# A rescheduled opening: a fused attention and feed-forward kernel whose first two batches are put into another order on every engine

## Chip, cores, metric

The kernel runs on one core of a Trainium2 chip. The metric is the device time of one execution in microseconds (us). Profiles (traces) are of one execution each; the span of a profile is shorter than the timed figure of the same execution (414.2 and 416.01 us for the kernel before). Engines: PE is TensorE, DVE is VectorE, ACT is ScalarE, POOL is GpSimd (which issues the loads), SP is SyncE.

## The reference

Attention over 8 batches, 8 heads, 576 positions, head dimension 64, with a bias that depends on the distance of two positions; then a bilinear feed-forward.

```python
scores = q @ k.T / 8 + bias          # per batch and head; bias from a table of 32 buckets
attn   = exp(scores - max); attn /= sum(attn)
x      = (attn @ v) rearranged to [4608 tokens, 512]
out    = ((x @ w_a) * (x @ w_b)) @ w_out          # w_a, w_b: 512 x 1536, w_out: 1536 x 512
```

## The kernel before

It works on 32 head pairs (four to a batch). The exp of the bias is a table W; scores go through exp on ACT and are multiplied by W on DVE. A load "lands" when the profile shows its end and whoever waits for it may start. The feed-forward of a chunk of 512 tokens is woven between the attention of later batches: groups of four matmuls "pa" (x times w_a) and "pb" (x times w_b), a copy "ha" on ACT, a product "g" on DVE, and output groups "po". The first chunk can start when batch 0 is through; until then PE is short of work. So the first 72 us are written down as a list of tokens, which is the order in which every engine gets its instructions:

```python
opening = """
    <k0 <q0 <q123h0 <tk <k23 <k1 <W0 <v0 <vtb <Wtb <W1 <W3 <vta <W2 <tq <R1 <q123h1 <v1 <R0 <Wta
    <wa0 <wb0 TK0 PD0 CK0:A PD1 w1 TQ0 PU1 CQ00:D CQ01:D w4 S000 w2 PU0 TQ20 E000 PC1 TQ10 S001 CQ20:D
    ...
    N00 TZ0 E301 M100 X00 S201 CX00:D AV10 wa4 E201 M200 N10 CZ0:A M201 X10 TQ11 M301 CX10:A T0 CQ11:A
    ...
    S310 CX20:A MT1 X30 E110 AV01 CX30:D M111 FA0a E310 M110 S210 FB0a N01 HA0a S211 E210 FA1a G0a
    AV11 HA1a M210 E211 X01 T2 N11 TZ0x CX01:A T3 ET2 FB1a M211 X11 FA2a G1a CX11:A S311 MT2 HA2a
    ...
"""
```

`<x` issues a load; `TQ`/`TK` are transposes of Q and K on PE, `CQ`/`CK` their copies (`:A` on ACT, `:D` on DVE); `S`, `E`, `M` scores, exp and product with the table; `T`, `ET`, `MT` the same for the 64 tail positions; `AV` probabilities times V, `N` its normalisation, `X` and `CX` the transposes and copies of x; `FA`, `HA`, `FB`, `G` the feed-forward (`a`, `b`: halves of 256 tokens, `f`: all 512); `w4` four dummy matmuls of 512 columns, `wa4` the same written to the bank of "av" (the results of `AV`); `PU`, `PC`, `PV`, `PF`, `PX`, `PD` zero fills. "pb" in this text is the first `FB`: from there on PE has the feed-forward as filling.

```python
    def load_weights(src, dst, part):                       # <wa0, <wb0: 512 KB each
        nc.gpsimd.dma_start(out=dst[part][:, :, :],
            in_=src[:, WC * part:WC * part + WC].rearrange("(m p) n -> p m n", p=128))
    ...
    def ff_o_out(c, tt):                                    # one output block of 128 tokens
        ob = wrk.tile([128, DM], FP32, tag="ob", name=f"ob{c}_{tt}")    # two buffers in turn
        nc.scalar.activation(out=ob[:, :], in_=ff["po", tt][:, :], func=ACTF.Copy)
        if c < B:
            r0 = S * c + 128 * tt
            nc.scalar.dma_start(out=out[r0:r0 + 128, :], in_=ob[:, :])
```

The softmax here doesn't subtract the row's maximum and nothing guards it: scores larger than these inputs give would overflow.

## Time and profile before

| | before |
|---|---|
| timed, median of 3 (range) | 417.34 (416.81 to 418.78) |
| timed, the profiled execution | 416.01 |
| span of the profile | 414.21 |
| matmuls, of these dummies | 3497, 22 |
| shape changes of the array | 177 |
| sum of PE's slots | 397.82 |
| first pb starts | 27.94 |
| first w_b block landed | 27.89 |

A slot is the time from one matmul's start to the next when nothing is waited for; "excess" is what a start comes later than its slot says. 1.2 us before the first matmul, the slots, the excess, and 4.2 us after the last matmul's start make up the span.

### The profile page before, as it was taken

The numbers are of one execution on the slowest core, as the hardware profiler recorded it, in microseconds if no ns is written. First come the engines' busy times: TensorE is split into PE (matmuls) and PEld (weight loads), VectorE is DVE, ScalarE is ACT, GpSimd is POOL, SyncE is SP. The second block draws the span as 40 slices with busy tenths as digits, with TensorE's granted clock in tenths as the row PEclk, the third lists the DMA queues.
The fourth block names the chain that finished last, engine by engine and source line by source line (L and its number), as shares of the span: only waits on it lengthen the run. The fifth ranks groups of instructions, "written<-read, shape, count | busy, mean of one in ns | idle before, by whom it ended". The sixth has DMA issues, their size and how long they took to land.

```text
span 414.2 us, 8826 instructions
## 1 busy us (share of the span) xinstructions
PE 403.8 (97%) x3497; PEld 210.9 (51%) x3497; DVE 241.1 (58%) x568; ACT 251.3 (61%) x388; POOL 133.5 (32%) x191
## 2 busy tenths in 40 slices
PE   8789999999999999999999999999999999999996
PEld 3467664545454455544555555554545555444443
DVE  5778887466764665477646774567646652421320
ACT  4988876486647676676667665866476742322321
POOL 7956546399209500870059003400000000000000
PEclk9999999999999999999999999999999999999999
DMA  9999999999949943996099707940421012002004
GB/s 116 171 210 191 205 157 144 164 142 138 123 96 163 121 82 71 150 128 112 15 162 157 112 16 140 124 92 17 101 82 16 17 40 78 0 2 102 1 2 101
DMA packets 135786, 42.05 MB, mean 102 GB/s; under 512 B 113688, under 2 KB 130968, under 8 KB 135744
## 3 DMA queue, kind: packets, MB, share of 16 engines
q0 software_dynamic: 81712, 20.27, 54.6%
q1 hardware_dynamic: 48592, 11.87, 18.1%
q10 hardware_dynamic: 5440, 9.34, 6.8%
q8 instruction: 27, 0.44, 0.5%
q14 instruction: 15, 0.12, 0.1%
HBM read 39.18 MB, written 9.45 MB: 117 GB/s over the span
## 4 chain that ended last, share of the span: by engine, by line
PE 90%; DMA 3%; POOL 2%; ACT 2%; issue 1%; ACTq 0%; DVE 0%
PE pb L633 23%; PE pa L633 23%; PE po L670 22%; PE av L569 7%; PE qk L406 7%; DMA wb<-in_moe_w_b_dram 3%; PE av L559 2%; PE av L563 2%; PE qkt L479 1%; POOL W L235 1%; DMA bias_tab<-wo 1%; PE trb L306 1%; PE trb L415 1%; PE warm L220 1%; ACT att L514 1%
## 5 line engine op out<-in xcount | busy, mean ns | idle before, releaser
L430 ACT ACTIVATE at<-qk 128x1024 bf16<-128x1024 f32 x112 | 113.5, 1030 | 26.4 <-PE qk L406 10.6
L643 DVE TENSOR_TENSOR g<-pb,ha 128x512 bf16<-128x512 f32 (+1 forms) x116 | 75.9, 654 | 74.7 <-PE pb L633 46.8
L633 PE MATMUL pb<-xn,wb 128*128 128x512 bf16 (+1 forms) x464 | 112.5, 365 | 0.8 <-DMA wb<-in_moe_w_b_dram 0.8
L633 PE MATMUL pa<-xn,wa 128*128 128x512 bf16 (+1 forms) x464 | 112.5, 365 | 0.0
L640 ACT ACTIVATE ha<-pa 128x512 f32<-128x512 f32 (+1 forms) x116 | 66.7, 575 | 65.0 <-PE pa L633 65.0
L670 PE MATMUL po<-wo,g 128*128 128x512 bf16 x420 | 99.0, 379 | 0.0
L435 DVE TENSOR_TENSOR at<-at,W 128x1024 bf16<-128x1024 bf16 x112 | 74.8, 684 | 18.2 <-ACT at L430 18.2
L633 PEld LDWEIGHTS <-wa 128*128 128x128 bf16 x464 | 42.0, 98 | 46.2 <-issue 6.0
L633 PEld LDWEIGHTS <-wb 128*128 128x128 bf16 x464 | 41.4, 97 | 43.0 <-issue 4.7
L670 PEld LDWEIGHTS <-g 128*128 128x128 bf16 x420 | 38.7, 98 | 44.0 <-issue 2.5
L675 ACT ACTIVATE ob<-po 128x512 f32<-128x512 f32 x35 | 21.1, 601 | 40.7 <-PE po L670 34.4
L569 PE MATMUL av<-vm,at 128*128 128x65 bf16 x896 | 41.2, 194 | 0.0
L170 POOL DMA_DIRECT2D vt<-in_v_dram x12 | 7.4, 621 | 104.1 <-PE av L563 103.2
L580 DVE RECIPROCAL rc<-av 128x6 f32<-128x6 f32 (+1 forms) x64 | 11.9, 186 | 49.5 <-PE av L569 43.8
L569 PEld LDWEIGHTS <-at 128*128 128x128 bf16 x896 | 37.2, 98 | 6.2
L132 POOL DMA_DIRECT2D qn<-in_q_dram x48 | 36.8, 832 | 9.9 <-PE pb L633 6.8
L141 POOL DMA_DIRECT2D kn<-in_k_dram x48 | 36.4, 820 | 2.0 <-PE pb L633 1.4
L559 PE MATMUL av<-vt,att 128*128 128x130 bf16 x152 | 33.3, 219 | 0.0
L406 PE MATMUL qk<-QB,KB 64*128 64x512 bf16 x192 | 29.2, 381 | 0.2 <-ACT att L506 0.2
L582 DVE TENSOR_TENSOR XG<-av,rc 128x384 bf16<-128x384 f32 (+1 forms) x64 | 27.1, 424 | 2.2
L506 ACT ACTIVATE att<-qkt 128x640 bf16<-128x640 f32 x24 | 16.9, 702 | 12.9 <-PE qkt L480 12.9
L559 PEld LDWEIGHTS <-att 128*128 128x128 bf16 x152 | 15.0, 98 | 6.4
(104 smaller groups left out, 325.2 us busy)
## 6 DMA issues: line engine op xcount, KB each, us to landing
out_dram<-ob ACTq DMA_DIRECT2D x32, 256.0 KB, 2.6
vn<-in_v_dram POOLq DMA_DIRECT2D x16, 256.0 KB, 5.6
kn<-in_k_dram POOLq DMA_DIRECT2D x48, 64.0 KB, 4.6
qn<-in_q_dram POOLq DMA_DIRECT2D x48, 64.0 KB, 4.3
wa<-in_moe_w_a_dram POOLq DMA_DIRECT2D x3, 512.0 KB, 9.3
wb<-in_moe_w_b_dram POOLq DMA_DIRECT2D x3, 512.0 KB, 10.4
wo<-in_moe_w_out_dram POOLq DMA_DIRECT2D x1, 1536.0 KB, 15.5
xn<-XG SPq DMA_TRANSPOSE x52, 4.1
```

Source lines behind the costliest of these rows:

```text
L132: nc.gpsimd.dma_start(out=by_tile(qn[b % 2])[:, h0 // 4, t, :, :], in_=q[b, h0:h1, 128 * t:128 * t + 128, :].transpose([1, 0, 2]))
L141: nc.gpsimd.dma_start(out=by_tile(kn[b % 2])[:, h0 // 4, t, :, :], in_=k[b, h0:h1, t:SM:NM, :].transpose([1, 0, 2]))
L406: nc.tensor.matmul(out=ps[:, hh, :], lhsT=kT[r, t, :], rhs=qT[r, :, :], start=True, stop=True)
L430: nc.scalar.activation(out=at[:, :, :], in_=ps[:, :, :], func=ACTF.Exp, scale=scale)
L435: nc.vector.tensor_tensor(out=at[:, :, :], in0=at[:, :, :], in1=w[:, :, S - 1 + t:S - 1 + t - SM:-1], op=MULT)
L559: nc.tensor.matmul(out=pav[:, slot, :, :], lhsT=weights_tail(p, jq), rhs=vt[i][:, hp, :, :], start=True, stop=True)
L569: nc.tensor.matmul(out=pav[:, slot, hh, :], lhsT=weights(p, t, hh, jq), rhs=vm[i][:, 2 * hp + hh, t, :], start=False, stop=True, skip_grou ...
L582: nc.vector.tensor_tensor(out=xg[:, jqs[0]:jqs[0] + m, :, :], in0=pav[:, 0:m, :, 0:Dh], in1=rc[:, 0:m, :].unsqueeze(3).to_broadcast([128, ...
L633: nc.tensor.matmul(out=ps[:, 0:n], lhsT=w[df // 4][:, mc, 128 * (df % 4):128 * (df % 4) + 128], rhs=xn_sb[mc][:, 512 * c + lo:512 * c + lo ...
L640: nc.scalar.activation(out=ha[:, 0:n], in_=ff["pa", df, lo][:, 0:n], func=ACTF.Copy)
L643: nc.vector.tensor_tensor(out=g_sb[df][:, lo:lo + n], in0=ff["pb", df, lo][:, 0:n], in1=ff["ha", df, lo][:, 0:n], op=MULT)
L670: nc.tensor.matmul(out=po[:, :], lhsT=g_sb[df][:, 128 * tt:128 * tt + 128], rhs=wo_sb[:, df, :], start=(df == 0), stop=(df == NDF - 1))
```

## The change

The intent: an automatic search (a list scheduler, then annealing) over the order of the whole opening up to the end of batch 1, of loads and of the instructions of every engine. What comes with it: 14 dummies instead of 22; work from behind the first pb in front of it; another load order; three of the zero fills moved to ACT, and those of the zero blocks (`PU`, `PF`) in 4-byte form; two more feed-forward groups per matrix no longer halved; the last head pair of batch 1 written as tokens instead of by the loop; and, as output blocks now come closer together, the third of chunk 0 in a buffer that is otherwise used only at the end.

```diff
-            parts = [(range(0, 8), 0, 256), (range(0, 8), 256, 256), (range(8, NDF), 0, 512)]
+            parts = [(range(0, 6), 0, 256), (range(0, 6), 256, 256), (range(6, NDF), 0, 512)]
...
-        ob = wrk.tile([128, DM], FP32, tag="ob", name=f"ob{c}_{tt}")
+        ob = ob_last if (c, tt) == (0, 2) else wrk.tile([128, DM], FP32, tag="ob", name=f"ob{c}_{tt}")
...
-        <k0 <q0 <q123h0 <tk <k23 <k1 <W0 <v0 <vtb <Wtb <W1 <W3 <vta <W2 <tq <R1 <q123h1 <v1 <R0 <Wta
-        <wa0 <wb0 TK0 PD0 CK0:A PD1 w1 TQ0 PU1 CQ00:D CQ01:D w4 S000 w2 PU0 TQ20 E000 PC1 TQ10 S001 CQ20:D
-        CQ10:D TQ30 E001 PC0 TZ1 CQ30:D S011 CZ1:A PC2 <vt1b <uq <vt1a <R2 <wa1 <q4 <R3 <k4 <wb1 <vb1b
...
+        <k0 <q0 <k1 <q123h0 <k23 <tk <W0 <v0 <W1 <vtb <vta <tq <W2 <R0 <v1 <Wta <q123h1 <W3 <Wtb <R1
+        <wa0 <k4 <wb0 <R2 <R3 <q4 <k5 <uq <q7 <q5 <wa1 <wb1 <k6 <uk <vt1b <k7 <vb1a <vb1b <vt1a <wa2 <q6
+        <wb2 <wo TK0 PC0:A TQ0 PF1:D PX1:D PV1:A PU0:D CK0:A CQ00:D w1 S001 PX0:D CQ01:A S000 E001 E000
+        w1 TQ30 PC1:D TK1 CK1:D TQ10 CQ10:D S011 E011 CQ30:D TK3 S100 E100 TZ1 CK3:D S301 M001 TQ20
+        PV0:D TK2 E301 S101 E101 CQ20:D CK2:D w1 S200 E200 CZ1:D M000 w1 KS w1 S201 EK w2 S010 E201 V0:D
...
+        MT0 AV01 CX20:D M110 E111 N30 ET1 X30 M111 CQ31:A T2 ET2 S210 CX30:D E210 PF0:A LH FA0a N01 HA0a
+        MT1 TK4 X01 T3 AV11 ET3 CX01:D S211 PU1:D FB0a FA1a E211 CK4:D HA1a N11 X11 G0a M210 S310 MT2
...
+        FB10f N70 HA10f G10f AV71 FA11f N71 FB11f X71 HA11f G11f AV61 N61 X70 FO00 FO01 FO02 HO0 CX70:D
+        CX71:D
...
-    for s in range(7, NP + 1):
+    for s in range(8, NP + 1):
```

Cut: the rest of the token list, the helpers for the zero fills (`pad`, `pad_blocks`), the new layout of `vt` and the loop code that the tokens replace.

More of the change, by code (lines that the diff above doesn't have):

```diff
@@ L95 @@
     vm = [wpool.tile([128, H, NM, Dh + 1], BF16, name=f"vm{i}") for i in range(2)]
-    vt = [wpool.tile([128, H // 2, 2, Dh + 1], BF16, name=f"vt{i}") for i in range(2)]
+    vt = [wpool.tile([128, 2, H // 2, Dh + 1], BF16, name=f"vt{i}") for i in range(2)]
     QT = [wpool.tile([128, NM, 128], BF16, name=f"QT{i}") for i in range(4)]
@@ L170, in load_vt @@
             nc.gpsimd.dma_start(
-                out=vt[b % 2][64 * hh:64 * hh + 64, :, hh, 0:Dh],
+                out=vt[b % 2][64 * hh:64 * hh + 64, hh, :, 0:Dh],
                 in_=v[b, hh:H:2, SM:S, :].transpose([1, 0, 2]))
@@ L191, in pad_tl, with pad, pad_vt, pad_blocks @@
         nc.vector.memset(tl[i][64:128, :, :, 0:Dh], 0.0)
-    def pad_vt(i):
-        nc.vector.memset(vt[i][0:64, :, 1, :], 0.0)
-        nc.vector.memset(vt[i][64:128, :, 0, :], 0.0)
+    def pad(eng, x, p0, p1):
+        if eng is nc.vector:
+            nc.vector.memset(x, 0.0)
+            return
+        n = int(np.prod(x.shape[1:]))
+        z = (zero_sb.bitcast(FP32) if x.dtype == FP32 else zero_sb)[p0:p1, 0:n]
+        if len(x.shape) == 3:
+            z = z.rearrange("p (a b) -> p a b", b=x.shape[2])
+        elif len(x.shape) == 4:
+            z = z.rearrange("p (a b c) -> p a b c", b=x.shape[2], c=x.shape[3])
+        nc.scalar.activation(out=x, in_=z, func=ACTF.Copy)
+    def pad_vt(i, hh, eng):
+        pad(eng, vt[i][64 * hh:64 * hh + 64, 1 - hh, :, :], 64 * hh, 64 * hh + 64)
+    def pad_blocks(x, hh, eng):
+        o = (Dh - Dh * hh) // 2
+        pad(eng, x.bitcast(FP32)[64 * hh:64 * hh + 64, :, :, o:o + Dh // 2], 64 * hh, 64 * hh + 64)
     def pad_ones(i):
-        nc.vector.memset(vt[i][0:64, :, 0, Dh:Dh + 1], 1.0)
-        nc.vector.memset(vt[i][64:128, :, 1, Dh:Dh + 1], 1.0)
+        nc.vector.memset(vt[i][0:64, 0, :, Dh:Dh + 1], 1.0)
+        nc.vector.memset(vt[i][64:128, 1, :, Dh:Dh + 1], 1.0)
         nc.vector.memset(vm[i][:, :, :, Dh:Dh + 1], 1.0)
-    def pad_x(i):
-        nc.vector.memset(XG[i][64:128, 4, :, :], 0.0)
+    def pad_x(i, eng):
+        pad(eng, XG[i][64:128, 4, :, :], 64, 128)
     nc.sync.dma_start(out=bt_sb[0:NB, :], in_=bias_table)
@@ L213 @@
     nc.vector.memset(tab_sb.bitcast(FP32)[0:H, :], TWO_ONES)
+    pad_ones(0)
+    pad_ones(1)
     nc.vector.tensor_tensor(out=bt_sb[0:NB, :], in0=bt_sb[0:NB, :], in1=bl_sb[0:NB, :],
@@ L240 @@
     nc.sync.dma_start(out=tab.ap(), in_=tab_sb[0:H, :])
-    pad_vt(0)
-    pad_ones(0)
     def load_wt(hh):
@@ L250, in load_vt_part @@
         nc.gpsimd.dma_start(
-            out=vt[b % 2][64 * hh:64 * hh + 64, :, hh, 0:Dh],
+            out=vt[b % 2][64 * hh:64 * hh + 64, hh, :, 0:Dh],
             in_=v[b, hh:H:2, SM:S, :].transpose([1, 0, 2]))
@@ L339, in copy_k @@
         copy(eng, KT[p % 4][:, :, :], st[p]["tk"][:, 0:SM].rearrange("d (t c) -> d t c", t=NM))
-    def t_q(p, eng=None):
-        if p >= NP or not early(p // 4):
-            return
-        ps = tr_half()
-        transposes(ps, qn, p)
-        copy(eng, QT[p % 4][:, :, :].rearrange("d a c -> d (a c)").rearrange("d (p t) -> d p t", t=NM),
-             ps[:, 0:SM].rearrange("d (t p) -> d p t", t=NM))
-    def t_k(p, eng=None, pool=None):
-        if p >= NP or not early(p // 4):
-            return
-        ps = pool.tile([128, 1024], BF16, tag="ffn", name=f"trk{p}") if pool else tr_half()
-        transposes(ps, kn, p)
-        copy(eng, KT[p % 4][:, :, :], ps[:, 0:SM].rearrange("d (t c) -> d t c", t=NM))
     tz = {}
@@ L559, in av_mm @@
             nc.tensor.matmul(out=pav[:, slot, :, :], lhsT=weights_tail(p, jq),
-                             rhs=vt[i][:, hp, :, :], start=True, stop=True)
+                             rhs=vt[i][:, :, hp, :], start=True, stop=True)
             if jq == 4:
@@ L593, in t_x @@
         c0 = SM * B + ST * b
-        if 4 <= p < NP - 1 and p != 7:
+        if 4 <= p < NP - 1:
             nc.sync.dma_start_transpose(
@@ L728 @@
     opening = """
-        <k0 <q0 <q123h0 <tk <k23 <k1 <W0 <v0 <vtb <Wtb <W1 <W3 <vta <W2 <tq <R1 <q123h1 <v1 <R0 <Wta
-        <wa0 <wb0 TK0 PD0 CK0:A PD1 w1 TQ0 PU1 CQ00:D CQ01:D w4 S000 w2 PU0 TQ20 E000 PC1 TQ10 S001 CQ20:D
-        CQ10:D TQ30 E001 PC0 TZ1 CQ30:D S011 CZ1:A PC2 <vt1b <uq <vt1a <R2 <wa1 <q4 <R3 <k4 <wb1 <vb1b
-        <q5 <k5 <uk <vb1a <wb2 <q6 <q7 <k6 <k7 <wa2 <wo S010 PF0 TK3 PF1 E011 TK2 CK3:D CK2:D E010 w1
-        S300 M001 TK1 E300 M000 KS CK1:D EK w1 S101 V0:D E101 w1 S100 E100 M101 w1 S200 AV00 M300 E200 S301
@@ L734 @@
-        N00 TZ0 E301 M100 X00 S201 CX00:D AV10 wa4 E201 M200 N10 CZ0:A M201 X10 TQ11 M301 CX10:A T0 CQ11:A
-        V1:D TQ31 ET0 S111 M010 AV20 E111 PW MT0 T1 N20 AV30 CQ31:A ET1 M011 TQ21 LH S110 N30 X20 CQ21:A
-        S310 CX20:A MT1 X30 E110 AV01 CX30:D M111 FA0a E310 M110 S210 FB0a N01 HA0a S211 E210 FA1a G0a
-        AV11 HA1a M210 E211 X01 T2 N11 TZ0x CX01:A T3 ET2 FB1a M211 X11 FA2a G1a CX11:A S311 MT2 HA2a
-        FB2a ET3 CZ0x:D AV21 G2a E311 M310 TQ4 FA3a N21 CQ4:A TK4 FB3a HA3a CK4:D X21 FA4a G3a CX21:A
@@ L739 @@
-        S41 M311 HA4a S43 E41 MT3 FB4a FA5a E43 G4a AV31 LV M41 HA5a S40 V3:D S42 N31 E40 FB5a TQ5 G5a
-        E42 X31 FA6a CQ5:D FB6a HA6a CX31:D TK5 G6a TZ1x CK5:A FA7a M40 FB7a HA7a CZ1x:D S52 S53 G7a E52
-        FA0b V2:D FB0b M42 HA0b T4 E53 G0b FA1b M52 FB1b HA1b S50 M53 ET4 FA2b G1b TQ6 M43 HA2b S51
-        CQ6:A FB2b MT4 E51 TQ7 G2b AV40 CQ7:D E50 TK6 M51 TK7 CK6:A FA3b M50 FB3b HA3b CK7:D S61 G3b T5
-        E61 N40 FA4b FB4b HA4b M61 T6 ET5 G4b AV41 FA5b ET6 N41 TH S63 FB5b MT5 HA5b S62 E63 FA6b G5b MT6
@@ L744 @@
-        AV50 HA6b M63 E62 S60 FB6b N50 E60 FA7b G6b AV51 M62 HA7b FB7b M60 FA8f G7b N51 FB8f HA8f G8f
+        <k0 <q0 <k1 <q123h0 <k23 <tk <W0 <v0 <W1 <vtb <vta <tq <W2 <R0 <v1 <Wta <q123h1 <W3 <Wtb <R1
+        <wa0 <k4 <wb0 <R2 <R3 <q4 <k5 <uq <q7 <q5 <wa1 <wb1 <k6 <uk <vt1b <k7 <vb1a <vb1b <vt1a <wa2 <q6
+        <wb2 <wo TK0 PC0:A TQ0 PF1:D PX1:D PV1:A PU0:D CK0:A CQ00:D w1 S001 PX0:D CQ01:A S000 E001 E000
+        w1 TQ30 PC1:D TK1 CK1:D TQ10 CQ10:D S011 E011 CQ30:D TK3 S100 E100 TZ1 CK3:D S301 M001 TQ20
@@ new lines @@
+        PV0:D TK2 E301 S101 E101 CQ20:D CK2:D w1 S200 E200 CZ1:D M000 w1 KS w1 S201 EK w2 S010 E201 V0:D
+        M101 TZ0 M100 M200 M201 AV00 N00 CZ0:A AV10 E010 X00 CX00:A S300 E300 N10 T0 V1:D X10 CX10:A
+        M010 ET0 AV20 TQ11 TQ21 M011 N20 CQ11:A S110 S111 CQ21:A E110 X20 M301 TQ31 M300 AV30 T1 PW:D
+        MT0 AV01 CX20:D M110 E111 N30 ET1 X30 M111 CQ31:A T2 ET2 S210 CX30:D E210 PF0:A LH FA0a N01 HA0a
+        MT1 TK4 X01 T3 AV11 ET3 CX01:D S211 PU1:D FB0a FA1a E211 CK4:D HA1a N11 X11 G0a M210 S310 MT2
@@ new lines @@
+        CX11:A E310 FB1a G1a S311 FA2a HA2a TQ4 M211 CQ4:A FB2a AV21 E311 FA3a HA3a TQ5 MT3 M310 S43 S42
+        CQ5:A G2a FB3a N21 M311 TK5 E43 E42 TZ0x G3a CZ0x:D AV31 LV CK5:D N31 FA4a HA4a X21 TQ7 CQ7:A
+        S41 E41 S52 E52 CX21:D FB4a FA5a HA5a X31 G4a TK6 M43 FB5a CX31:D S40 E40 S53 G5a FA0b FB0b
+        CK6:D M41 TZ1x HA0b G0b CZ1x:D S51 FA1b FB1b E53 M53 HA1b G1b E51 TK7 CK7:D M40 FA2b HA2b S50
+        E50 FB2b FA3b G2b HA3b V2:D T4 FB3b FA4b V3:D ET4 G3b S70 E70 M42 MT4 M52 HA4b FB4b G4b TQ6 T5
@@ L745 @@
+        ET5 M50 CQ6:A AV40 N40 MT5 M51 FA5b S71 E71 HA5b S73 FB5b AV41 G5b M70 N41 S72 E73 FA6f E72 T6
+        M73 M71 HA6f FB6f G6f AV50 N50 S62 ET6 MT6 E62 S61 FA7f HA7f M62 AV51 N51 TH S60 E61 M61 FB7f
+        G7f E60 M60 S63 E63 M63 FA8f HA8f M72 T7 FB8f G8f AV60 N60 ET7 MT7 FA9f HA9f FB9f G9f AV70 FA10f
+        FB10f N70 HA10f G10f AV71 FA11f N71 FB11f X71 HA11f G11f AV61 N61 X70 FO00 FO01 FO02 HO0 CX70:D
+        CX71:D
     """
@@ L819, in step @@
             av_norm(p, jqs)
-            if not first and i[1] == 1:
+            if 4 <= p < 7 and i[1] == 1:
                 t_x(p)
@@ L825, in step @@
             copy_x(p, jqs, eng)
+        elif kind == "PV":
+            pad_vt(0, p, eng)
+        elif kind == "PC":
+            pad_vt(1, p, eng)
         elif kind == "PU":
-            pad_z(1, p)
+            pad_blocks(ZB[1], p, eng)
         elif kind == "PF":
-            nc.vector.memset(tl[0][64 * p:64 * p + 64, :, :, Dh - Dh * p:128 - Dh * p], 0.0)
-        elif kind == "PC":
-            if p == 2:
-                pad_ones(1)
-            else:
-                nc.vector.memset(vt[1][64 * p:64 * p + 64, :, 1 - p, :], 0.0)
+            pad_blocks(tl[0], p, eng)
+        elif kind == "PX":
+            pad_x(p, eng)
         elif kind == "PW":
-            nc.vector.tensor_copy(out=Wt_sb[:, :, 0:64], in_=Wt_sb[:, :, 64:128])
-        elif kind == "PD":
-            pad_x(p)
+            copy(eng, Wt_sb[:, :, 0:64], Wt_sb[:, :, 64:128])
         elif kind == "LH":
@@ L851 @@
     pad_tl(1)
-    quotas = {7: 9, 8: 9}
     load_slot = {bb: 9 if bb == 3 else 12 if bb == 4 else 4 * bb - 5 for bb in range(3, B)}
-    for s in range(7, NP + 1):
+    for s in range(8, NP + 1):
         new = s < NP
         U = "unit"
-        A = lambda *jq: (lambda: av(s - 1, jq))
+        A = lambda *jq: (lambda: av(s - 1, jq) if s > 8 else None)
         steps = []
@@ L862 @@
         if new:
-            head = [U, lambda: ex(s, 1), A(0, 1, 2), U, lambda: mul(s, 0), lambda: t_q(s + 1), U,
+            head = [U, lambda: ex(s, 1), A(0, 1, 2), U, lambda: mul(s, 0), U,
                     lambda: mul(s, 1)]
@@ L866 @@
             if s == 8:
-                late = [A(3, 4), U, lambda: t_x(7, (0, 1, 2)), U, lambda: t_x(7, (3, 4))]
-            if shared(s):
-                pair = [lambda: v_next(s), lambda: (qk(s, 2), ex(s, 2), ex_rows(s)), U,
-                        lambda: ex(s, 3), U, lambda: mul(s, 2), lambda: mul_rows(s)]
-            else:
-                pair = [lambda: v_next(s), lambda: (qk(s, 2), ex(s, 2)), U, lambda: ex(s, 3),
-                        lambda: t_k(s + 1, ACT), U, lambda: mul(s, 2)]
+                late = [U]
+            pair = [lambda: v_next(s), lambda: (qk(s, 2), ex(s, 2), ex_rows(s)), U,
+                    lambda: ex(s, 3), U, lambda: mul(s, 2), lambda: mul_rows(s)]
             tail = [lambda: (qk_tail(s), ex_tail(s)), U, U, lambda: mul_tail(s)]
@@ L893 @@
                     load_half(bb, g)
-        quota = quotas.get(s, 9)
+        quota = 9
         seen, put = 0, 0
```

## The prediction

> **What bounds the kernel now.** I read the page first, for the engine that is full, then the chain of waits in order of time, to see where TensorE (PE) is not what holds the end, then PE's waits, then sums by stretch. The page:
>
> ```profile
> PE 403.8 (97%) x3497; PEld 210.9 (51%) x3497; DVE 241.1 (58%) x568; ACT 251.3 (61%) x388; POOL 133.5 (32%) x191
> ...
> PE 90%; DMA 3%; POOL 2%; ACT 2%; issue 1%; ACTq 0%; DVE 0%
> ```
>
> PE is the bound on 90% of the chain; no other engine passes 61%. Most of the 10% that is not PE lies in one piece at the start, as the chain in order of time shows (start, length, what; us):
>
> ```profile
> 4.29 2.50 DMA bias_tab<-wo
> ...
> 16.69 0.75 POOL wa L255
> 17.43 10.46 DMA wb<-in_moe_w_b_dram
> 27.89 0.05 issue
> 27.94 0.61 PE pb L633 x4
> ...
> 46.59 0.44 PE pb L633 x4
> 47.03 0.32 PE qk L406 x2
> 47.35 0.54 PE pa L633 x4
> ```
>
> Up to 27.9 us the end hangs on the load queue: the first block of w_b lands at 27.89 and releases the first "pb" group. From there to the end it is PE. The sums by stretch (PE is the first busy column) agree:
>
> ```profile
> 0.00:28.00 28.00, 22.56 (x299) 12.74 (x300) 20.61 (x63) 20.95 (x30) 20.69 (x33) 1.00 1.13 159
> 28.00:72.00 44.00, 43.22 (x513) 28.94 (x514) 36.46 (x94) 33.02 (x56) 27.50 (x38) 1.00 1.50 177
> 72.00:414.00 342.00, 337.99 (x2688) 169.26 (x2685) 184.02 (x412) 197.37 (x303) 85.29 (x120) 1.00 0.68 87
> ```
>
> PE is idle 5.4 of the first 28 us and 0.8 of the next 44. The single waits are small:
>
> ```profile
> PE qkh L446 <- ACT ath L452: 1.2, 2, 1.0
> PE warm L220 <- DVE zero_sb L212: 1.2, 1, 1.2
> PE pb L633 <- DMA wb<-in_moe_w_b_dram: 0.8, 1, 0.8
> ```
>
> Busy time flatters PE, so I used starts. From one start to the next in the trace, a matmul of 512 columns takes 0.216 us, of 256 0.109, of 130 0.057, of 65 0.0325, of 128 0.056; two half-array ones of 64 rows share a slot. Whenever the array shape changes, 0.095 us is added: above, four matmuls of 256 columns ("pb") take 0.44 after full-array work, and the four "pa" after a "qk" group 0.54. Summing such slots over the whole instruction order gives 397.8 us. The rest of the 414.2 is 1.2 before the first matmul, 7.4 of excess up to the first pb (27.94), 3.5 after it, and 4.2 after the last matmul's start. Of the 3.5, single gaps above 0.15 us between 34 and 57 us make 1.5, one at 85 makes 0.4, and the rest is spread thinly.
>
> **What the Trainium skill says.** "TensorEngine Tiling (Array Packing)", Tiling Modes, Key Properties: "Changing tiling mode (not just tile) drains the TensorE". The trace agrees: the 0.095 us. "TensorE: Matmul & The Clock Gate", Part 1, says that PE starts at half clock, is released after about 3.4 us of activity and falls back after an idle window of that length. The trace agrees on the start: the first five fill-up matmuls are 0.43 us apart, later ones 0.216. That is why dummy matmuls stand in the opening, and why taking some out has a risk. "DMA: Bandwidth & Descriptors", Issuing engines are not separate DMA queues, says that all loads share the same 16 engines; so a new order of loads moves a landing only by the bytes put before it. The trace agrees: from 5 to 56 us loads land one after another, 128 KB every 0.65 to 0.75 us, 512 KB every 2.5 to 3.5 us.
>
> **The change, part by part.**
>
> 1. Matmuls removed. The built orders differ, apart from order, by 8 dummy matmuls of 512 columns (22 before, 14 after), and 32 of 256 columns that become 16 of 512 (df 6 and 7 are no longer halved). The dummies are worth 8 x 0.216 = 1.73 us of slots. The merging is worth nothing: 2 x 0.109 = 0.218 against 0.216.
>
> 2. Shape changes: 177 before, 170 after; 7 x 0.095 = 0.67 us. So the slot sum falls from 397.8 to 395.4 us.
>
> 3. Where it falls. Up to the first pb both orders hold 19.3 us of slots. There the change takes out 1.73 of dummies and 4 shape changes (0.38), and puts in work that stood later: the tail scores of head pairs 2 and 3 (2 x 0.39), the second half of AV of pair 1 (0.92), one batch 1 K transpose (0.23) and three transposes of X (0.17), together 2.1. So work moves from the PE-bound stretch into one where PE has 7.4 us to spare. From the first pb on, 376.1 us are left instead of 378.5: **2.4 us less**.
>
> 4. When the first pb starts. Its w_b block stays behind the same 20 loads and now also behind a K load of batch 1 (128 KB, 0.65 us); Wta, last of those 20, landed at 21.46, w_a took 2.9 and w_b 3.5. So it lands at about 21.5 + 2.9 + 0.65 + 3.5 = 28.5: **0.6 us later**. ScalarE should not be later than that. Its exps follow each other every 0.90 us; before this pb it has 13 half exps, one for the tail keys and three tails of 0.9 (15.3), two copies at 0.38, five at 0.28 (2.2): 17.5 us. With a first exp near 7.0 (7.41 before; 4 dummies no longer stand ahead of the first scores) that is 24.5, plus perhaps 1 to 1.5 of gaps. The zero fills moved to ScalarE sit in its idle time before 5.4 or are one of 0.4 us. I expect PE to wait for w_b 1 to 2.5 us, longer than the 0.8 of now.
>
> 5. After it. From starts and slots, the second w_b block is wanted at 28.5 + 9.4 = 37.9. Loads ahead of it now: R2, R3, five q, k and tail loads (about 3.9 us together), then w_a and w_b (2.45 + 3.37 in this trace), so it lands near 38.3: a new wait of about 0.4. The other gaps of 34 to 57 us (1.5 now) come from copies that PE waits for; a better order should halve them, 0.7. Together 1.1.
>
> 6. Third output block in its own buffer. Output blocks 0 to 2 now follow each other more closely; with two buffers block 2 would wait for block 0's store, some 4 us from issue to landing. This only keeps a ScalarE wait away: 0. Transposes of pair 7 stay on PE; same count.
>
> 7. Zero fills in ScalarE and 4-byte form, vt laid out anew: off the path, 0.
>
> Sum: 28.5 + 376.1 + excess after it (1.1 + 0.4 at the first shared steps + 1.6 spread = 3.1) + 4.2 = 411.9 us against 414.2 in the profile, so 2.3 less. The timed median of 417.34 becomes **415.0**.
>
> **Rivals.**
>
> A. The load queue takes it all back. For: w_b comes 0.6 later by my count, the second one is 0.4 short, and the fourth head pair waits for its table load, which landed at 15.5 and, behind what now stands ahead of it, should land near 19.9; VectorE works in order and would hold everything behind it. Against: the bytes before each are nearly the same, and 2.4 us of PE work is gone from behind it. If all waits came out 1 us worse, 416.
>
> B. ScalarE holds the opening, not the loads. For: it was without a gap from 10 to 20 us (9.7 of 10 busy). Then the first pb starts when the exps are through; if PE, too, is fed late, 29 to 30, and the time is 416 to 417. Against: two of its copies (the tail keys, 2 x 0.38) leave the gap before the third exp for VectorE, where ScalarE now loses 0.5 + 0.8 us.
>
> C. The clock falls back without the dummies between 6 and 8 us. For: six leave there. Against: PE still has something every microsecond, and the idle window is 3.4 us. It would cost about 1.5, all of it in slack or after it: 415 to 416.5.
>
> D. The order was fitted to measured durations, and the landing is earlier than I add up, or the gaps of 34 to 57 vanish wholly: 412.5 to 414.
>
> **Range and chances.** The gain of 2.4 us is a sum of removed slots and firm; what is open is the first pb (28 to 29.5) and the excess after it (2 to 4.5), each about 1 us, and the timing's own spread (416.81 to 418.78 for one kernel). So 413.2 to 416.8. 2% would be 8.3 us: faster by that would need all excess of the opening gone, slower would need a new stall of 10 us that no view hints at: 0.02 and 0.01.
>
> **What would show it.** Right: 3473 matmuls; a last matmul about 2.3 us earlier; first pb at 28 to 29 released by the w_b load with a PE wait above 1 us; granted clock 1.00 in the first 28 us; the chain still loads up to there and PE afterwards; PE idle from 28 to 72 at most 0.8; from the start of batch 2 the two traces equal but for the shift. Wrong: first pb released by ScalarE or DVE, or later than 29.5; a PE wait on the second w_b or on a transposed batch 2 load above 1 us; a clock below 1; or a stretch after 85 us that differs in length.

## The result

The kernel after took 413.74 us (median of 6, 413.25 to 414.45), the kernel before 417.07 beside it (median of 6, 416.21 to 418.78). The ratio is 0.9919, 95% interval 0.9896 to 0.9942: 0.8% less, inside the 2% band, 1.3 us below the figure predicted and inside its range.

The page of the kernel after, engines and chain:

```profile
PE 404.5 (98%) x3473; PEld 210.0 (51%) x3473; DVE 240.8 (58%) x568; ACT 251.3 (61%) x384; POOL 133.6 (32%) x191
...
PE 94%; DVE 2%; ACT 2%; DMA 1%; issue 1%; ACTq 0%; POOL 0%; POOLq 0%
```

The matmuls are the 3473 that were counted. PE carries 94% of the chain instead of 90%, and loads 1% instead of 3%. The chain of waits in order of time (start, length, what), where it leaves the first load, and around the first pb:

```profile
2.06 4.09 DMA qn<-in_q_dram
...
13.99 1.94 ACT ath L452 x2
...
19.64 0.89 DVE vm L313
20.52 1.20 DVE ath L461 x2
...
21.86 0.41 ACT QT L311
22.27 0.04 issue
22.31 0.61 PE qkh L446 x8
...
29.18 0.33 PE qkh L446 x4
29.51 0.54 PE pb L633 x4
```

Before, one piece of 10.46 us read "DMA wb" and ended at the first pb. Here the w_b load is not in the chain: it landed at 28.68, and the first pb started at 29.44 (the chain splits its pieces a little later than the starts). From 22.31 on everything is PE's own work, except for 0.02 of issue. Before that come exps, products and copies that follow one from another. This is one execution; in the traces of runs 3, 5, 11 and 12, whose opening is the same or all but the same, the load comes last (run 5).

The sums by stretch, with PE as the first busy column:

```profile
0.00:28.00 28.00, 24.51 (x308) 14.12 (x309) 20.13 (x60) 21.36 (x30) 21.53 (x34) 1.00 1.05 158
28.00:72.00 44.00, 44.00 (x530) 28.34 (x528) 38.69 (x108) 33.64 (x54) 27.73 (x39) 1.00 1.53 177
```

PE is busy 24.5 of the first 28 us instead of 22.6, and all of the next 44 instead of 43.2. PE's waits (who waited for what: us in total, times, longest):

```profile
PE warm L237 <- DVE zero_sb L227: 1.2, 1, 1.2
PE trb L321 <- DMA qn<-in_q_dram: 0.9, 1, 0.9
PE qkh L446 <- ACT QT L311: 0.6, 1, 0.6
PE trb L609 <- DVE XG L582: 0.5, 1, 0.5
PE pb L633 <- DVE g L643: 0.2, 1, 0.2
```

No wait for w_b is among them. Starts and slots give the whole account (us):

| | before | after | difference |
|---|---|---|---|
| slots up to the first pb | 19.33 | 19.32 | 0.0 |
| excess up to the first pb | 7.42 | 8.93 | +1.51 |
| slots after it | 378.5 | 376.1 | -2.41 |
| excess, first pb to first scores of batch 2 (73 us) | 1.86 | 0.58 | -1.28 |
| excess after that | 1.74 | 1.86 | +0.12 |
| span | 414.21 | 412.16 | -2.05 |

The profiles differ by 2.05 us, the timed medians by 3.3. That is no contradiction: the profile of the kernel before was an early one of its kind. Over the 11 executions beside the first set of experiments its spans were 414.0 to 415.9 (mean 415.06); the kernel after's were 411.4 to 412.7 in two sets of six (mean 412.0). That is 3.1 us. The experiments below find what varies: the landing of w_b.

### The profile page after: what moved, and what is told of

It is laid out like the page before. It is cut to its first block, busy times and chain, and to the rows that moved or that the text cites. A ratio compares the mean times of both kernels' runs of the same rounds, so it can differ in the third digit from the quotient of the medians. Undisturbed runs are those within 1.5% of the kernel's fastest.

```text
span 412.2 us, 8768 instructions
## 1 busy us (share of the span) xinstructions
PE 404.5 (98%) x3473; PEld 210.0 (51%) x3473; DVE 240.8 (58%) x568; ACT 251.3 (61%) x384; POOL 133.6 (32%) x191
## 4 chain that ended last, share of the span: by engine, by line
PE 94%; DVE 2%; ACT 2%; DMA 1%; issue 1%; ACTq 0%; POOL 0%; POOLq 0%
PE pb L633 23%; PE pa L633 23%; PE po L670 22%; PE av L569 8%; PE qk L406 7%; PE av L559 2%; PE av L563 2%; PE qkh L446 1%; PE qkt L479 1%; DMA qn<-in_q_dram 1%; PE trb L321 1%; ACT ath L452 1%; PE trb L415 1%; PE trb L609 0%; DVE ath L461 0%
## 5 line engine op out<-in xcount | busy, mean ns | idle before, releaser
L582 DVE TENSOR_TENSOR XG<-av,rc 128x384 bf16<-128x384 f32 (+2 forms) x64 | 27.2, 425 | 2.2
```

Source lines behind the costliest of these rows:

```text
L582: nc.vector.tensor_tensor(out=xg[:, jqs[0]:jqs[0] + m, :, :], in0=pav[:, 0:m, :, 0:Dh], in1=rc[:, 0:m, :].unsqueeze(3).to_broadcast([128, ...
```

## The experiments

Twelve kernels, in three calls of four; each call on one chip, with its own runs of the kernel before beside it (416.78, 416.87 and 416.65 us, medians of 11). "Before" and "after" in a heading say which kernel was edited. All gave the right result. Where the trace of a later run lacks some 50 PE records, I used starts and landings from it, not sums of slots.

### 1. The kernel before, again (ctl_before)

No edit.

> The kernel before against itself. The timed medians fell by 3.3 us, the two profiled spans by 2.0. Theory L: the kernel before hangs on the landing of the first w_b block (27.89 us in its trace), and that landing moves from run to run, so its spans spread upwards: 414 to 416, with the first pb group at 27.9 to 29.5. Rival: the spans of before lie within 0.5 us of 414.2, and the missing 1.3 us is outside the program (launch or timer). Ratio 1.000 in both.

Measured: 416.85 us, ratio 0.9999 (0.9981 to 1.0016). Its profile has a span of 414.93, with w_b landed at 28.61. Span less landing is 386.32; in the first profile of this kernel it was 414.21 - 27.89 = 386.32 as well, and in run 2 below 415.50 - 29.17 = 386.33. So in all three profiles the kernel before takes the landing of w_b plus a constant, and the difference between their spans is that of this landing.

### 2. Before, without eight dummies (b_dummies_out)

```diff
-  ... CQ00:D CQ01:D w4 S000 w2 ...        ... AV10 wa4 E201 ...
+  ... CQ00:D CQ01:D S000 w2 ...           ... AV10 E201 ...
```

> The kernel before without 8 of its 22 dummy matmuls (four before the first scores, four at 18.7 us). Theory (they stood in time that the loads set, so taking them out frees nothing by itself): ratio 0.999 to 1.001, first pb at 27.9 or wherever the first w_b block lands, granted clock 1.00. Rival 1 (the dummies are the gain): 1.7 us less, ratio 0.996. Rival 2 (without them the clock falls back): 1.5 us more, clock below 0.99 in the first 28 us.

Measured: 416.98 us, ratio 1.0002 (0.9986 to 1.0019). Taking out 8 x 0.216 = 1.73 us of PE work gained nothing: it all stood ahead of the load that sets the first pb. The sums by stretch (the third number from the right is the granted clock) show that they had kept the clock up:

```profile
8.00:12.00 4.00, 3.69 (x57) 2.21 (x54) 2.55 (x12) 2.83 (x5) 3.54 (x6) 0.61 0.86 119
12.00:16.00 4.00, 3.49 (x32) 1.75 (x29) 2.93 (x7) 3.59 (x4) 4.00 (x7) 0.53 1.15 179
```

PE ran at little over half clock for 8 us, and that cost nothing either, as PE had so much time to spare there.

### 3. After, with the eight dummies put in behind the first pb (a_dummies_late)

```diff
-  ... S60 E61 M61 FB7f
+  ... S60 E61 M61 wa8 FB7f
```

> The changed kernel with 8 dummy matmuls of 512 columns put in at about 61 us. Theory (from 22 us on PE's slots are the time): 8 x 0.216 = 1.7 us more than the changed kernel, ratio to before about 0.996; the trace shows the last matmul 1.7 later. Rival (some later wait sets the end and absorbs them, the next at the 224 us gap or the stores): no more than 0.5 us more.

Measured: 416.33 us, ratio 0.9986 (0.9970 to 1.0003), so 2.7 us more than the kernel after, against 1.7 expected. The same 1.73 us of work that cost nothing in front costs its full length behind the first pb, and more. PE's waits show part of the surplus:

```profile
PE fill L237 <- DVE XG L587: 0.6, 1, 0.6
```

My dummies wanted the one bank of "av", which DVE had not read out yet. That is a fault of the experiment, not of the theory. In the profile the span less first pb is 385.12, 2.4 more than in the kernel after: 1.73 of dummies and this wait.

### 4. After, with some of the work that had been drawn forward put back (a_work_late)

```diff
-  MT1 TK4 X01 T3 AV11 ET3 CX01:D S211 PU1:D FB0a FA1a ...
+  MT1 S211 PU1:D FB0a TK4 X01 T3 AV11 ET3 CX01:D FA1a ...
```

> The changed kernel with a batch 1 K transpose, three X transposes, the tail scores of pair 3 and the second AV half of pair 1 (1.7 us of slots) moved back from before to behind the first pb group. Theory (what is before the first pb is free only as far as the w_b load leaves room): PE arrives at 27.7, waits for the load that landed at 28.68, so the first pb starts at 28.7 to 28.8 instead of 29.44, with 1.7 more left to do: 1.0 us more (0.6 to 1.4) than the changed kernel, and a PE wait on w_b of about 1 us. Rival (only the sum of slots counts): within 0.3 us of the changed kernel.

Measured: 416.86 us (415.35 to 418.29), ratio 0.9992 (0.9965 to 1.0020): 3.1 us more than after, three times what I expected. The six spans fall into two groups: 413.6, 413.7 and 414.2 with a mean clock of 0.995 to 0.999, and 416.0, 416.5 and 416.5 with 0.987 to 0.995. The first group lies 1.9 us above the kernel after. The slots moved are 1.7 us (K transposes 0.23, transposes of x 0.17, tail scores 0.39, AV 0.92), which is about that. The profile, of the second group, shows the rest. A line of PE's timeline (start, length, engine and line, operation, tiles and shapes, count; in brackets the idle time before it and what ended it) and the sums by stretch:

```profile
29.99 0.73 PE L633 MATMUL pb<-xn,wb 128*128 128x256 bf16 x4 [1.47 <-DMA wb<-in_moe_w_b_dram]
```

```profile
28.00:32.00 4.00, 2.41 (x24) 1.60 (x24) 1.47 (x7) 1.67 (x4) 2.10 (x4) 0.79 1.45 217
32.00:36.00 4.00, 3.61 (x42) 2.70 (x39) 2.36 (x9) 1.91 (x3) 3.98 (x6) 0.78 1.21 184
```

With less work in front, PE ran into the w_b load and waited 1.5 us, and then its clock fell just where every microsecond of PE counts: the four pb matmuls after the wait show a length of 0.73 us, a pb group at 35.61 in the same timeline, with the clock back, 0.61. So work in front of the first pb leaves less to do behind. That it also keeps PE's clock up to the landing is what this profile suggests; it is not shown, as an execution with the same mean clock, 0.995, has a span of 414.2 and not 416.5.

### 5. The kernel after, again (ctl_after)

No edit.

> The changed kernel unchanged, for the others of this call and for its own spread. Expected: ratio 0.992, span 411.4 to 412.7, first pb at 29.4 (not on the w_b load, which lands at about 28.7).

Measured: 413.66 us, ratio 0.9920 (0.9904 to 0.9936). In its profile w_b landed at 29.27 and the first pb started at 29.31. Span less first pb is 382.76; in the first profile of this kernel, where PE's own work was last, it is 382.72. The chain of this run has the load again, as in the kernel before:

```profile
19.12 10.14 DMA wb<-in_moe_w_b_dram
29.27 0.05 issue
29.31 0.61 PE pb L633 x4
```

PE waited 0.34 us for w_a at 25.99 and 0.32 for w_b here, so the expectation "not on the w_b load" missed. It is the same in runs 3, 11 and 12: the first pb starts 0.05 us after the landing (29.22, 29.69, 28.76), after PE waits for w_a of 0.2 to 0.65 and for w_b of 0.2 to 0.3. So the first pb of the kernel after hangs on two things, the load and the chain of work. In these five profiles they end within 0.8 us of each other, and the load is last in four. What is behind the first pb is constant in the two profiles of the unchanged kernel.

This also gives the whole account. Behind the first pb the kernel after needs 382.7 us instead of 386.27, so 3.55 less. With the mean spans of 415.06 and 412.0, an estimate of the mean first pb is 28.8 before and 29.3 after, so 0.5 later. Together that is the 3.1 us.

### 6. After, with the load order of before (a_loads_old)

```diff
-  <k0 <q0 <k1 <q123h0 <k23 <tk <W0 <v0 <W1 ... <wa0 <k4 <wb0 <R2 <R3 <q4 <k5 ...
+  <k0 <q0 <q123h0 <tk <k23 <k1 <W0 <v0 <vtb ... <wa0 <wb0 <vt1b <uq <vt1a <R2 <wa1 <q4 <R3 <k4 ...
```

> The changed kernel with the loads in the order of before. Theory (the new order of PE needs the new order of loads): the K transpose of pair 4 stands before the first pb, and its load, moved back behind the second w_a block and two more, lands at about 33 instead of 26, so PE stands still from about 27 to 33 and the kernel loses most of it: 3 to 5.5 us more than the changed kernel, slower than before. Rival (the order of loads hardly matters, all are bytes in one queue): within 0.7 us of the changed kernel.

Measured: 422.79 us, ratio 1.0129 (1.0108 to 1.0150): 9 us more than after, against 3 to 5.5 expected. PE's waits name the load that comes too late, K of the first pair of batch 1:

```profile
PE trb L321 <- DMA kn<-in_k_dram: 4.8, 1, 4.8
```

w_b itself landed earlier (27.58), but the first pb started at 38.01, since `TK4` stands ahead of it in PE's order. The clock fell as well, to 0.68 from 32 to 36 us and 0.50 from 36 to 40.

### 7. Before, with the load order of after (b_loads_new)

```diff
-  <k0 <q0 <q123h0 <tk <k23 <k1 <W0 <v0 <vtb <Wtb <W1 <W3 ... <wa0 <wb0 TK0 ...
+  <k0 <q0 <k1 <q123h0 <k23 <tk <W0 <v0 <W1 <vtb <vta <tq <W2 <R0 <v1 <Wta <q123h1 <W3 ... <wa0 <k4 TK0 ...
```

> The kernel before with the loads in the new order. Theory: VectorE wants the table of pair 3 at 17.4 and gets it at about 20.5, so everything in order behind it is held, and the first w_b block lands 0.8 later: 1 to 3 us more than before, ratio 1.002 to 1.007. Rival (the new order of loads alone is the gain): 1 us or more less than before.

Measured: 420.76 us, ratio 1.0088 (1.0072 to 1.0105): 3.9 us more than before, against 1 to 3 expected. DVE's timeline names the cause:

```profile
20.70 0.69 DVE L461 TENSOR_TENSOR ath<-ath,W 128x1024 bf16<-128x1024 bf16 x1 [3.03 <-DMA W<-bias_tab]
```

The table of the fourth head pair landed at 20.68 and the old order of products wanted it 3 us earlier; DVE takes its instructions in order, so PE then waited 3.4 us for a normalisation behind it. Runs 6 and 7 together: neither half of the change, the load order or the instruction order, works without the other. In the kernel after the same table landed at 20.52, and nothing waited for it, because its product stands later.

### 8. After, with the Q load of three pairs ahead of a K load (a_q_first)

```diff
-  <k0 <q0 <k1 <q123h0 <k23
+  <k0 <q0 <q123h0 <k1 <k23
```

> The changed kernel with the half load of Q for pairs 1 to 3 ahead of the K of pair 1 again, as in before. There Q of pair 0 landed at 5.51, here at 6.16. Theory (the load behind it takes its bandwidth): it lands near 5.5 again, the first scores and the first exp are 0.4 to 0.6 earlier, and the first pb, which hangs on ScalarE and VectorE, comes 0.3 to 0.6 earlier; it can't be before the w_b landing of 28.7. So 0.3 to 0.6 us less than the changed kernel. Rival (later table loads or the keys set the products anyway): the first exp earlier, the end the same within 0.2.

Measured: 413.87 us, ratio 0.9921 (0.9904 to 0.9938): the same as after. The first exp started at 7.24, in the unchanged kernel at 8.01 and 7.33. So the later first exp in the profile of after is chance of one run, not an effect of the order, and the time does not hang on it. In the profile of this run the clock fell to 0.50 from 12 to 16 us, and the first pb came at 29.59, 0.65 after its load.

### 9. After, with w_b loaded before K of batch 1 (a_k4_late)

```diff
-  <wa0 <k4 <wb0        ... MT1 TK4 X01 T3 AV11 ...  FB0a FA1a E211 CK4:D
+  <wa0 <wb0 <k4        ... MT1 X01 T3 AV11 ...      FB0a FA1a TK4 E211 CK4:D
```

> The kernel after with the first w_b block loaded ahead of the batch 1 K load (0.65 us earlier) and that pair's K transposes (8 matmuls, 0.23 us) moved behind the first pb and second pa. Theory 'the first pb hangs on the w_b load, as in the kernel before': landing near 28.0 to 28.7, first pb 0.5 to 0.7 us earlier (28.7 to 28.9), 0.23 us of slots more behind it, net 0.2 to 0.5 us less than the unchanged kernel after, near 413.3. Rival 'in the kernel after the chain of PE, exps and copies is as late as the load (from 22.3 us on PE has almost no gap up to the first pb)': w_b lands earlier, but the first pb comes only some 0.3 earlier by the slots that left, span less first pb grows by 0.2, and the time is 413.6 to 413.9, the same.

Measured: 415.38 us, ratio 0.9962 (0.9945 to 0.9980): 1.6 us more than after; both expectations missed. In the profile w_b landed at 27.01, 1.7 us earlier than in the kernel after, and the first pb nevertheless started only at 30.29. So in this run the w_b load does not hold the first pb; the chain of work does (PE had waited 1.2 us for a Q load near 9 us, and the chain came later). Behind it my edit made a new wait, which the timelines of PE and DVE show:

```profile
32.77 0.59 PE L609 MATMUL trb<-ident,XG 128*128 128x128 bf16 x3 [1.09 <-DVE XG L582]
```

```profile
31.72 0.42 DVE L313 COPY KT<-trb 128x512 bf16<-128x512 bf16 x1 [1.83 <-PE trb L321]
```

The copy `CK4` stands in DVE's order ahead of a normalisation. By moving the transposes I made DVE stand still for 1.83 us, and PE waited 1.09 for what came behind. Span less first pb is 384.21, 1.5 more than in the kernel after: 0.23 of slots moved, the rest this wait and its followers. Run 10 has the same edit, the same two waits (1.85 on DVE, 1.08 on PE) and 384.26. So the loss is nearly all what I put behind the first pb, above all the new wait, and this run can't tell what the place of the K load is worth.

### 10. The same, and without five dummies near 15 us (a_k4_no_fill)

```diff
-  CK2:D w1 S200 E200 CZ1:D M000 w1 KS w1 S201 EK w2 S010      (beside the edit of run 9)
+  CK2:D S200 E200 CZ1:D M000 KS S201 EK S010
```

> The same as the run with the K load behind w_b, and the five dummy matmuls between 13.8 and 16.8 us taken out as well (1.08 us of slots, all ahead of the first pb). Theory 'only PE work behind the first pb counts': the time of the run above within 0.3 us, as those slots stand where PE waits for exps. Rival 'the dummies stand in PE's chain': up to 0.6 us less. Rival 'they keep the clock up': a granted clock below 0.9 somewhere between 12 and 24 us and 0.3 to 3 us more.

Measured: 415.71 us (413.45 to 416.74), ratio 0.9963 (0.9937 to 0.9989): by the median the same as run 9, but the spread is larger, and it goes with the clock. The six spans with their mean clocks: 411.7 (0.998), 412.4 (0.994), 413.4 (0.992), 414.5 (0.984), 414.8 (0.984), 415.0 (0.983). The profile, of the third:

```profile
12.00:16.00 4.00, 2.45 (x23) 1.13 (x20) 3.77 (x10) 4.00 (x5) 4.00 (x7) 0.75 1.10 151
16.00:20.00 4.00, 4.00 (x55) 3.25 (x52) 3.26 (x8) 3.10 (x6) 4.00 (x7) 0.50 1.23 206
```

In the execution that kept its clock the span is below all of run 9 (412.6 to 414.5 there); the three that lost most are up to 3.3 us above it. So these dummies may stand in part in PE's chain, but that rests on one or two executions, and the landing of w_b moves too (29.10 in this profile, 27.01 in that of run 9, in the same order of loads). That the dummies keep the clock up agrees with these six spans. In the kernel before a like loss of clock cost nothing (run 2). That the kernel after has too little spare time in the opening to hide it is argued, not tested.

### 11. After, with three zero fills back on DVE (a_pads_dve)

```diff
-  PC0:A ... PV1:A ... PF0:A
+  PC0:D ... PV1:D ... PF0:D
```

> The kernel after with three zero fills (two of the tail V blocks, one of the batch 2 tail block) back on VectorE. My prediction's step 7 gave the move to ScalarE no worth: 413.6 to 413.9, ratio to the kernel before 0.992, first exp unchanged within 0.3 us. Rival 'VectorE is short in the opening and the fills delay its copies of QT and KT': first exp or first pb 0.3 to 0.6 later and the time 0.3 to 0.6 us more.

Measured: 413.84 us, ratio 0.9927 (0.9911 to 0.9943): the same. The engine of these fills is worth nothing that could be seen. In this profile w_b landed at 29.64, and PE waited 0.3 us for it; the span was 412.1 all the same.

### 12. After, with the third output block back in the two-buffer pool (a_ob_pool)

```diff
-  ob = ob_last if (c, tt) == (0, 2) else wrk.tile([128, DM], FP32, tag="ob", name=f"ob{c}_{tt}")
+  ob = wrk.tile([128, DM], FP32, tag="ob", name=f"ob{c}_{tt}")
```

> The kernel after with chunk 0's third output block back in the pool of two buffers. My prediction's step 6 gave the extra buffer no time of its own: ScalarE waits for the first block's store (some 3 to 4 us from issue to landing) but PE keeps two banks for it: 413.6 to 414.0. Rival 'the wait holds ScalarE and with it the exps that PE waits for next': a ScalarE wait above 1 us at the third output copy and 0.5 to 2 us more.

Measured: 415.74 us, ratio 0.9979 (0.9959 to 0.9999): 2.0 us more than after by the medians, and about 2.5 by the ratios (0.9979 - 0.9920 of 416.7); the rival is right. ACT's timeline in the kernel after and in this one:

```profile
80.17 0.62 ACT L675 ACTIVATE ob_last<-po 128x512 f32<-128x512 f32 x1
```

```profile
81.91 0.60 ACT L675 ACTIVATE ob<-po 128x512 f32<-128x512 f32 x1 [2.31 <-DMA out_dram<-ob]
```

And PE, two microseconds later in this run:

```profile
84.00 0.39 PE L406 MATMUL qk<-QB,KB 64*128 64x512 bf16 x2 [1.85 <-ACT at L430]
```

The store of the first block was issued at 73.37 and landed at 81.83: 8.5 us. In the kernel before a store in that place took 3.9 us (74.42 to 78.36) and the third copy came at 81.45, so two buffers were enough. In the kernel after the blocks come closer (copies at 73.44, 76.67, 80.17) and the first store takes 6.8 us. Without the third buffer ACT stands still, the next exp is late, and PE, which has only two banks of scores, waits 1.85 us.

## Why the prediction was right or wrong

**Slots (steps 1 to 3): right.** 3473 matmuls, 14 dummies, 170 shape changes, 2.41 us less behind the first pb. Run 2 shows that the removed dummies by themselves are worth nothing, run 3 that as much work behind the first pb costs at least its length, run 4 (its three shorter executions, 1.9 us for 1.7 us of slots) that this part of the gain is the work drawn forward into their place. The 0.67 us of fewer shape changes and the unhalved groups were counted, not tested by a run of their own.

**First pb (step 4): the landing was right, PE's wait for it was not.** I put w_b at 28.5; it landed at 28.68. But I expected PE to wait 1 to 2.5 us for it, and in this profile it did not wait: the first pb started at 29.44. In the four other profiles the load released it, as I said, but PE had waited for it only 0.2 to 0.3 us (and 0.2 to 0.65 for w_a before). I had added up ACT's exps and copies and one load, and never PE's own work behind the last of them, nor the products on DVE. The chain shows what I left out: DVE and ACT in turn up to 22.27, and then 7.1 us of PE without a gap, from 22.31 to the first pb. This is part of rival B, with its first pb of 29 to 30, but with PE's own work at the end and not the exps. Its time of 416 to 417 was wrong: it holds the same last step as the sum below. The premise that a landing moves only by the bytes ahead of it was also too strong: in runs 9 and 10, with the same order of loads, w_b landed at 27.01 and 29.10.

**Excess after it (step 5): mis-sized.** I put 3.1 (1.1 + 0.4 + 1.6); it measures 0.58 + 1.86 = 2.44. The new wait of 0.4 on the second w_b did not come: the block landed at 37.61, as its own transfer took 2.55 us and not 3.37, and it was wanted only at 39.09. (In run 5 it landed at 38.97 and its group started at 39.01, so there is no room to spare.) And the waits for copies between 34 and 57 us did not halve but all but vanished: before there were gaps of 0.22, 0.21, 0.27, 0.31 and 0.22 us, after there is none over 0.12, and those of 0.10 to 0.12 stand at score groups in both kernels. (The five sum to 1.2; the prediction's 1.5 was misread.) That was rival D's "the gaps of 34 to 57 vanish wholly". That its 412.5 to 414 holds the result is luck in part, as it too rests on the last step below. These 1.28 us are read from the traces of the two kernels alone. No run puts the old order of copies back by itself, so which move removed which gap stays open.

**Third buffer (step 6): the mechanism right, my size of the store wrong.** I said that it only keeps a wait away, and took the store as some 4 us. With copies 1 and 3 6.7 us apart, a store of 4 us would have made no wait at all. It was 6.8 us in the kernel after and 8.5 in run 12, and the wait kept away costs 2 to 2.5 us: some two thirds of the change's gain would be lost without this one line. The text had no number for that.

**Zero fills (step 7): right for the engine of three of them** (run 11). The 4-byte form and the new layout of `vt` were not tested.

**The sum and its last step.** The sum for the profiled span was 411.9; it was 412.16, as the first pb came 0.9 later than the sum's 28.5 and the excess was 0.7 smaller. That these two errors nearly cancel is luck. The step that put the time 1.3 us too high is the last: "The timed median of 417.34 becomes 415.0". I took the difference of two spans from the median of other executions. The profiled execution itself had been timed at 416.01, so timed less span was 1.8, and 411.9 + 1.8 = 413.7, which is what came. The kernel before spreads with its landing, and its profile was at the early end.

**The other rivals.** A, the load queue takes it back: no, in runs of the whole change; runs 6 and 7 show that it would have with either half of it. C, the clock falls back: not in this profile of the kernel after (granted 1.00 throughout), but in three of its six timed executions the mean clock was 0.990 or 0.991. The profile of run 8, with a mean of 0.989, shows what that can be: 0.88, 0.50 and 0.77 in the three windows from 8 to 20 us. The mean of those three spans is 412.3, of the other three 411.8, so it cost little. With run 5, six of twelve executions of the kernel after have a mean clock under 0.996; of the 33 of the kernel before beside the runs, two have. In runs 4 and 10 a fall went with a longer time.

**What stays open.** Why the same load in the same queue lands up to 2 us apart from run to run. Nor did any run show how little activity makes the clock fall: run 9 had 2.82 of 4 us busy from 8 to 12 us and kept it, run 8 had 2.89 and lost it.

## What to carry to other kernels

Where one load or one chain releases the stretch in which PE is full, count PE's slots on each side of that point: here, work taken out in front of it was worth nothing, and work drawn from behind it to the front was worth its length. Dummies in front could be exchanged for real work, but the clock then fell in more of the executions. Then follow every engine's chain to that point, PE's own included, before naming the load as its cause. When blocks come closer together, look again at buffers that were just enough: the third buffer was worth 2 us here, as the store took longer than assumed. And carry a predicted span to a time by the profiled execution's own time, not by a median of others.

## What the Trainium skill lacked or had wrong

- "TensorEngine Tiling (Array Packing)", Tiling Modes, Key Properties, says that a change of tiling mode drains TensorE, and gives no size. In these traces it is 0.095 us per change; with 177 and 170 changes it made 0.67 us of the 2.41 us that left the slots.
- "TensorE: Matmul & The Clock Gate", HAM oscillation, gives "no PE-idle gaps >~3.4µs" as the rule, and a later section tells of micro-idles without a figure. Here the clock went to half after much shorter gaps: in run 10 no gap of PE from 5 to 16 us was over 0.74 us, and none over 1.6 even if the transposes are not counted as work, and the granted clock was 0.75 from 12 to 16 us and 0.50 from 16 to 20; in run 4 a single wait of 1.47 us was followed by 0.79 and 0.78. The same kernel loses it in some executions and not in others.
- "DMA: Bandwidth & Descriptors", Anatomy of one DMA, fits the time of a transfer issued from GpSimd as 2.0 us and its bytes at 436 GB/s, and has no fit for one from ScalarE; for the 256 KB of an output block the formula would give an estimate of 2.6 us. The store of the first block took 3.9 us from issue to landing in the kernel before, 6.8 in the kernel after and 8.5 in run 12, beside loads in flight.
- No page tells how much the landing of one load varies. The first w_b block of the kernel before landed at 27.89 and 28.61 in two profiles, that of the kernel after at 28.68 and 29.27; for the kernel before, the end of the run moves with it one for one.
